# A gated MLP's two projections with their last 64 rows packed side by side, a written instruction order, and Wd's gradient split around dh

## The chip, the cores and the metric

The kernel runs on one core of one Trainium2 chip. The metric is the device time of one execution in microseconds (us); the time given for a version is the median of its runs.

## The reference, cut to what matters

The reference is the gradient of an attention block whose output is gated by a small MLP, for S = 2048 positions, D = 576 features, F = 4608 hidden features and 32 heads of 128. All tensors are bf16. The part that the change touches is the forward MLP and the gradients that belong to it:

```python
xn = _layernorm(x, axis=-1)
s = _A_ref(xn, k_cache, v_cache, wq, wo)      # attention
g = jnp.einsum("bsd,df->bsf", xn, w_gate)
u = jnp.einsum("bsd,df->bsf", xn, w_up)
h = _sigmoid(g) * u
gate = _silu(jnp.einsum("bsf,fd->bsd", h, w_down))
out = x + s * gate
```

The outputs are `out` and the gradients with respect to x, the two caches, wq, wo, w_gate, w_up and w_down.

## The kernel before

Everything runs on one core, stage after stage. D = 576 is four full tiles of 128 and a rest of 64 (`DT` = 5 tiles, `DL` = 4 full ones, `KL` = 64). The rest tile is padded: `zpad` (L158 to 160) clears rows 64 to 127 of the fifth tile of `xnT`, `wg_sb` and `wu_sb`, so that its matmul can use all 128 rows of the array, half of them with zeros.

**Stage 1, the projections (L177 to 263).** The 2048 positions are 16 row blocks (`st`). Each is layer-normed by `ln_tile` (L206 to 221): VectorE's statistics over two halves (L211, L213), a square root on ScalarE (L215), a reciprocal and a bias on VectorE (L216, L219), the normalisation itself on ScalarE (L220), and five TensorE transposes (L59) whose result is copied to `xnT` by VectorE (the four full tiles) and ScalarE (the rest). F is nine chunks of 512 in three groups of three. For each group, each row block and each chunk, a *unit* computes g and u: five matmuls of 128x512 into a PSUM bank for g (L249) and five for u (L252). ScalarE then makes sigmoid(g) (`a_row`, L253) and sigmoid(-g) (`oma`, L255); VectorE makes h = u * a (L256) and b = h * oma (L257). After three chunks the rows h, a and b are stored to DRAM from Pool's DMA queue (L259, L262, L263). There are 144 units. PSUM has three pairs of banks for them. Rows and small tiles have two or three buffers.

Loads of x and the weights are issued on SP (L183, L194, L195, L197): the first two row blocks of x, the first chunk of both weights, the other 14 row blocks in one transfer, then the rest of group 0 and groups 1 and 2. Wd's load (`wd_sb`, L236) and the store of the normed x (L235) are written at the last row block of group 0. The order of the instructions on each engine is the scheduler's here, which may move an instruction ahead of where it is written.

**Stage 2 (L267 to 325)** multiplies h, read back transposed (`hT`, L261 and L282), with Wd (L306). It reads the last tile of `xnT`, whose upper half (rows 64 to 127) it overwrites with the transposed rest of another tensor (`transpose_ds`). Then the **attention stage** runs over the heads, by far the longest, with an order written by hand for TensorE, VectorE and ScalarE. A stage over the row blocks follows (L723), and its transposes `transpose_doB` (L669).

**The stage of the MLP's weight gradients (L740 to 825)** goes over 18 blocks of 256 hidden features (`fb`). In each, `make_dh` (L776) computes dh and from it `du_blk` and `dg_blk` on VectorE (L781, L782); `make_dwd` (L794) computes two tiles of Wd's gradient (`fl` 0 and 1) from `h_blk` and `doB`; then come the gradients of Wu and Wg (`accw`, L811) and, for their last 64 rows, `accl` (L819), which puts du's into columns 0 to 63 of the array and dg's into columns 64 to 127. In the first block make_dwd goes ahead of make_dh, with the last three `transpose_doB` inside it; in the others it is the other way round. `load_abh` loads h, a and b of a block, `h_blk` on Pool's queue except for the first block. Only SP keeps its written order in this stage. The scheduler puts the first 20 matmuls of dh ahead of the first dWd tile in the first block.

Of the kernel before, what the change touches and what calls it, by code (L numbers as in the profile page):

```python
# [9 lines left out]
bf = mybir.dt.bfloat16  # L10
# [3 lines left out]
P = 128  # L14
# [81 lines left out]
def kernel(  # L96
# [77 lines left out]
    zpad(xnT)  # L174
    dsT = pk.tile([P, DL, S], bf, name="dsT")
    wo_h = pk.tile([P, D], bf, name="wo_h")
    with tc.tile_pool(name="pa", bufs=1) as pa:  # L177
        wd_sb = pa.tile([P, FT, D], bf, name="wd_sb")
        with tc.tile_pool(name="a1w", bufs=1) as wp:
            a0x = tc.alloc_tile_pool(name="a0x", bufs=1, side="right")  # L180
            x_all = a0x.tile([P, NT, D], bf, name="x_all")
            XF = min(2, NT)
            nc.sync.dma_start(x_all[:, 0:XF, :], x2[0:XF * P, :].rearrange("(t p) d -> p t d", p=P))  # L183
            xn_st = x_all
# [5 lines left out]
            bounds = [0, FCH] + list(range(WSPL, F + 1, WSPL)) if WSPL > FCH else list(range(0, F + 1, WSPL))  # L190
            for bi in range(len(bounds) - 1):
                c0, c1 = bounds[bi], bounds[bi + 1]
                for i, (d0, kd) in enumerate(dts):
                    nc.sync.dma_start(wg_sb[:kd, i, c0:c1], B_w_gate[d0:d0 + kd, c0:c1])  # L194
                    nc.sync.dma_start(wu_sb[:kd, i, c0:c1], B_w_up[d0:d0 + kd, c0:c1])  # L195
                if bi == 0 and NT > XF:
                    nc.sync.dma_start(x_all[:, XF:, :], x2[XF * P:, :].rearrange("(t p) d -> p t d", p=P))  # L197
# [4 lines left out]
            with tc.tile_pool(name="a0", bufs=3) as sb0, tc.tile_pool(name="a0ps", bufs=2, space=PSUM) as ps0, \  # L202
                    tc.tile_pool(name="a1r", bufs=2) as rows, tc.tile_pool(name="a1t", bufs=3) as tmpp, \
                    tc.tile_pool(name="a1ps", bufs=3, space=PSUM) as ps:

                def ln_tile(st):  # L206
                    xt = x_all[:, st, :]
                    stats = sb0.tile([P, nchunk, nc.vector.BN_STATS_DIM], f32, name="stats")
                    xr = xt.rearrange("p (c f) -> p c f", c=nchunk)
                    for c in range(nchunk):  # L210
                        nc.vector.bn_stats(stats[:, c, :], xr[:, c, :])  # L211
                    mv = sb0.tile([P, nc.vector.BN_AGGR_DIM], f32, name="mv")
                    nc.vector.bn_aggr(mv[:], stats[:])  # L213
                    std = sb0.tile([P, 1], f32, name="std")
                    nc.scalar.activation(std[:], mv[:, 1:2], AF.Sqrt, bias=eps_t[:], scale=1.0)  # L215
                    nc.vector.reciprocal(rstd_all[:, st:st + 1], std[:])  # L216
                    xn_t = xn_st[:, st, :]
                    nbias = sb0.tile([P, 1], f32, name="nbias")
                    nc.vector.scalar_tensor_tensor(nbias[:], mv[:, 0:1], -1.0, rstd_all[:, st:st + 1], op0=ALU.mult, op1=ALU.mult)  # L219
                    nc.scalar.activation(xn_t, xt, AF.Identity, bias=nbias[:], scale=rstd_all[:, st:st + 1])  # L220
                    transpose_to(nc, ps0, xn_t, D, xnT, st * P, ident, alt)

                LA = 2
                for st in range(min(LA, NT)):
                    ln_tile(st)
                for grp in range(NFC // GRP):
                    if grp == 1:
                        a0x.release()
                        hp0 = tc.alloc_tile_pool(name="a2h0", bufs=1, side="right", reuse_waits="tile")
                        hT = {k: hp0.tile([P, FT, P], bf, name=f"hT{k}") for k in range(2)}  # L230
                    for st in range(NT):
                        if grp == 0 and st + LA < NT:
                            ln_tile(st + LA)
                        if grp == 0 and st == NT - 1:
                            nc.gpsimd.dma_start(xn_d[:, :].rearrange("(t p) d -> p t d", p=P), xn_st[:])  # L235
                            nc.gpsimd.dma_start(wd_sb[:], B_w_down.rearrange("(t p) d -> p t d", p=P))  # L236
                        srows = slice(st * P, (st + 1) * P)
                        a_row = rows.tile([P, GRP * FCH], bf, name="a_row")
                        b_row = rows.tile([P, GRP * FCH], bf, name="b_row")
                        h_row = rows.tile([P, GRP * FCH], bf, name="h_row")  # L240
                        for c in range(GRP):
                            fc = grp * GRP + c
                            fs = slice(fc * FCH, (fc + 1) * FCH)
                            cs = slice(c * FCH, (c + 1) * FCH)
                            g_ps = ps.tile([P, FCH], f32, name="g_ps")
                            u_ps = ps.tile([P, FCH], f32, name="u_ps")
                            for i, (d0, kd) in enumerate(dts):
                                kk = kfull(i, kd)
                                nc.tensor.matmul(g_ps[:], lhsT=xnT[:kk, i, srows], rhs=wg_sb[:kk, i, fs], start=(i == 0), stop=(i == DT - 1))  # L249
                            for i, (d0, kd) in enumerate(dts):  # L250
                                kk = kfull(i, kd)
                                nc.tensor.matmul(u_ps[:], lhsT=xnT[:kk, i, srows], rhs=wu_sb[:kk, i, fs], start=(i == 0), stop=(i == DT - 1))  # L252
                            nc.scalar.activation(a_row[:, cs], g_ps[:], AF.Sigmoid)  # L253
                            oma = tmpp.tile([P, FCH], bf, name="oma")
                            nc.scalar.activation(oma[:], g_ps[:], AF.Sigmoid, scale=-1.0)  # L255
                            nc.vector.tensor_tensor(h_row[:, cs], u_ps[:], a_row[:, cs], op=ALU.mult)  # L256
                            nc.vector.tensor_tensor(b_row[:, cs], h_row[:, cs], oma[:], op=ALU.mult)  # L257
                        cols = slice(grp * GRP * FCH, (grp + 1) * GRP * FCH)
                        nc.gpsimd.dma_start(h_d[srows, cols], h_row[:])  # L259
                        if grp == NFC // GRP - 1 and st in hT:  # L260
                            nc.sync.dma_start_transpose(hT[st][:], h_d[srows, :])  # L261
                        nc.gpsimd.dma_start(a_d[srows, cols], a_row[:])  # L262
                        nc.gpsimd.dma_start(b_d[srows, cols], b_row[:])  # L263

# [395 lines left out]
    if True:  # L660
# [80 lines left out]
        with tc.tile_pool(name="b1o", bufs=2, reuse_waits="tile") as outp, tc.tile_pool(name="b1t", bufs=3, reuse_waits="tile") as tmpp, \  # L741
# [21 lines left out]
            for fb in range(F // FB):  # L763
# [22 lines left out]
                def make_dwd():  # L786
                    for fl in range(FB // P):
                        frows = slice(fb * FB + fl * P, fb * FB + (fl + 1) * P)
                        accs = [psa.tile([P, 512], f32, name=f"accd{j}") for j in range(len(ncs))]
                        for st in range(NT):  # L790
                            if (fl, st) in ((0, NT // 2), (1, 4), (1, 12)) and pend_tr:
# [196 lines left out]
```

## Time and profile before

| what | value |
|---|---|
| median of 3 runs | 5172.25 us (5167.11 to 5178.84) |
| the profiled execution, its own time | 5193.94 us |
| span of the profiled execution | 5192.2 us |
| mean granted TensorE clock | 0.993 |
| TensorE busy | 5002.7 us (96%) |
| weight loads | 3622.5 us (70%) |
| VectorE busy | 3251.7 us (63%) |
| ScalarE busy | 2293.4 us (44%) |
| Pool busy | 1448.0 us (28%) |

How to read it: the span is that of one execution taken by the hardware profiler, and all rows of the trace are times inside it, counted from its start. PE is TensorE, PEld its weight loads, DVE VectorE, ACT ScalarE, POOL GpSimd, SP the engine that only issues DMAs; a q behind a name means the issuing of a DMA. L with a number is a line of the kernel. A row of the order of time gives start, duration, engine, line, operation, output and inputs; neighbours of one kind are merged, "x4" being their number. Matmuls are pipelined, so the durations of neighbours overlap, and the distance between two starts is the time that one takes of the engine. A few per cent of the matmul records are missing from a trace, so counts come from the code. In square brackets stands how long the engine was idle ahead of the row and what ended it.

### The profile page before, as it was taken

The page shows a single profiled execution, that of the slowest core. Times are in us where ns is not written, and L with a number is a line of the kernel's source. Part 1 is how long each engine was busy: PE and PEld are TensorE (multiplying, and loading weights), DVE is VectorE, ACT ScalarE, POOL GpSimd, SP SyncE. Part 2 cuts the span into 40 slices and gives each one's busy share as a digit, 9 for nine tenths or more (in the row PEclk, how much of TensorE's full clock was granted, in tenths as well). Part 3 has the DMA queues.
Part 4 walks back from the last instruction along what each step waited for, and adds up shares of the span by engine and source line. Part 5 has one row for each costly group of instructions (what it writes and reads, how often), then busy time and mean ns, then how long its engine had stood idle before and what let it go on. Part 6 is the DMA issues. An engine that isn't in the chain of part 4 may idle for free.

```text
span 5192.2 us, 127341 instructions
## 1 busy us (share of the span) xinstructions
PE 5002.7 (96%) x54402; PEld 3622.5 (70%) x55312; DVE 3251.7 (63%) x5099; ACT 2293.4 (44%) x2922; POOL 1448.0 (28%) x2110
## 2 busy tenths in 40 slices
PE   7999999999999999999999999999899999999999
PEld 3444777777777777777777777777757777754554
DVE  4545887888888888888888888888733222210111
ACT  6541665565566556655655665565501222100000
POOL 2222233233233323322332333233222333211000
PEclk8999999999999999999999999999999999999999
DMA  7477999999999999999999999999999776697775
GB/s 270 183 214 167 188 193 193 198 199 196 193 198 196 188 202 199 195 196 191 197 196 197 197 196 200 196 194 199 208 197 248 202 202 190 200 242 162 154 148 122
DMA packets 2712489, 1013.48 MB, mean 195 GB/s; under 512 B 2525424, under 2 KB 2646000, under 8 KB 2711920
## 3 DMA queue, kind: packets, MB, share of 16 engines
q1 hardware_dynamic: 2628256, 726.57, 81.3%
q0 software_dynamic: 83664, 278.71, 18.2%
q8 instruction: 432, 7.08, 0.6%
q14 instruction: 137, 1.12, 0.1%
HBM read 172.54 MB, written 201.00 MB: 72 GB/s over the span
## 4 chain that ended last, share of the span: by engine, by line
PE 84%; DMA 6%; DVE 5%; issue 4%; SPq 0%; ACT 0%; DVEq 0%; ACTq 0%; another core or an unknown queue 0%
PE acckv L544 17%; PE acc L525 14%; PE acc L929 7%; PE dp L495 6%; PE sp L465 5%; PE accw L811 5%; PE accp L424 4%; DVE sneg L467 4%; PE u_ps L252 3%; PE dh L776 3%; PE g_ps L249 3%; DMA dST<-dSq 3%; PE acc L306 3%; PE accd L794 3%; PE acc L867 2%
## 5 line engine op out<-in xcount | busy, mean ns | idle before, releaser
L476 ACT ACTIVATE Pq<-sneg,nm 128x2048 bf16<-128x2048 bf16 x512 | 1024.5, 2001 | 391.6 <-DVE sneg L467 388.5
L525 PE MATMUL acc<-Kn,dST 128*128 128x128 bf16 x8192 | 1068.5, 220 | 31.6 <-DMA dST<-dSq 29.8
L544 PE MATMUL acckv<-dOn,Pq 128*128 128x128 bf16 x8192 | 1032.7, 219 | 15.2
L525 PE MATMUL acc<-Vn,PT 128*128 128x128 bf16 x8192 | 1023.2, 219 | 14.7 <-DMA PT<-Pq 12.9
L498 DVE SCALAR_TENSOR_TENSOR dSq<-dp,delta,Pq 128x1024 bf16<-128x1024 f32 x608 | 774.2, 1281 | 361.9 <-PE dp L495 253.0
L544 PE MATMUL acckv<-Qn,dSq 128*128 128x128 bf16 x8192 | 899.5, 220 | 8.5 <-issue 0.2
L525 PEld LDWEIGHTS <-dST 128*128 128x128 bf16 x8192 | 759.6, 98 | 167.4 <-DMA dST<-dSq 38.3
L544 PEld LDWEIGHTS <-Pq 128*128 128x128 bf16 x8192 | 793.6, 98 | 117.1 <-issue 0.5
L525 PEld LDWEIGHTS <-PT 128*128 128x128 bf16 x8192 | 766.1, 98 | 156.0 <-DMA PT<-Pq 17.3
L544 PEld LDWEIGHTS <-dSq 128*128 128x128 bf16 x8192 | 721.0, 98 | 100.3 <-issue 1.1
L467 DVE TENSOR_SCALAR_CACHE_REDUCE sneg<-sp,nm 128x1024 bf16<-128x1024 f32 x512 | 656.6, 1282 | 83.3 <-PE sp L465 46.6
L467 DVE TENSOR_SCALAR_CACHE_REDUCE sneg<-sp 128x1024 bf16<-128x1024 f32 x512 | 625.3, 1221 | 59.4 <-PE sp L465 41.8
L501 ACT ACTIVATE t<-dp,negdelta 128x1024 bf16<-128x1024 f32 x416 | 463.6, 1114 | 431.1 <-PE acc L525 242.7
L465 PE MATMUL sp<-KT,QT 128*128 128x512 bf16 x1763 | 547.2, 379 | 33.2 <-DVE sneg L467 26.4
L495 PE MATMUL dp<-VT,dOT 128*128 128x512 bf16 x1728 | 541.5, 380 | 0.5 <-DVE dSq L498 0.5
L484 POOL TENSOR_TENSOR dOn<-dOn,rinv_all 128x256 bf16<-128x256 bf16 x256 | 155.9, 609 | 658.8 <-DVE rinv_all L480 541.7
L505 DVE TENSOR_TENSOR dSq<-t,Pq 128x1024 bf16<-128x1024 bf16 x416 | 319.4, 768 | 0.0
L811 PEld LDWEIGHTS <-xn_all 128*128 128x128 bf16 x2304 | 225.0, 98 | 31.6 <-DMA xn_all<-xn_d 3.1
L929 PEld LDWEIGHTS <-cf 128*128 128x128 bf16 x2304 | 145.9, 98 | 143.5 <-DMA cf<-dg_d 5.0
L942 DVE SCALAR_TENSOR_TENSOR junk<-dxn,xn_all 128x576 f32<-128x576 f32 x16 | 12.1, 758 | 372.8 <-ACT dxn L937 372.8
L591 POOL DMA_DIRECT2D dq_d<-dq_n x128 | 98.7, 771 | 478.6 <-DVE dq_n L590 470.2
L465 PEld LDWEIGHTS <-QT 128*128 128x128 bf16 x2048 | 163.1, 98 | 52.6 <-issue 50.8
(182 smaller groups left out, 6925.0 us busy)
## 6 DMA issues: line engine op xcount, KB each, us to landing
out_dram<-kv POOLq DMA_DIRECT2D x256, 128.0 KB, 5.0
h_d<-h_row POOLq DMA_DIRECT2D x48, 384.0 KB, 2.7
a_d<-a_row POOLq DMA_DIRECT2D x48, 384.0 KB, 2.6
b_d<-b_row POOLq DMA_DIRECT2D x48, 384.0 KB, 3.2
a_blk<-a_d SPq DMA_DIRECT2D x18, 1024.0 KB, 5.8
b_blk<-b_d SPq DMA_DIRECT2D x18, 1024.0 KB, 21.8
du_d<-du_blk POOLq DMA_DIRECT2D x18, 1024.0 KB, 8.4
dg_d<-dg_blk POOLq DMA_DIRECT2D x18, 1024.0 KB, 11.5
```

The lines of the kernel that those rows point to most:

```text
L424: nc.tensor.matmul(acc[:], lhsT=w[:, i, :], rhs=srcT[:, i, cs], start=(i == 0), stop=False)
L465: nc.tensor.matmul(sp[:, c * CH:(c + 1) * CH], lhsT=hs.QT[:, qs], rhs=hs.KT[:, hf * HW_ + c * CH: hf * HW_ + (c + 1) * CH], start=True, st ...
L467: nc.vector.tensor_scalar(sneg[:, hf * HW_:(hf + 1) * HW_], sp[:], -SCALE, None if hf == 0 else nm[:, hf - 1:hf], op0=ALU.mult, op1=ALU.mi ...
L476: nc.scalar.activation(Pq[:], sneg[:], AF.Exp, bias=nm[:, hf:hf + 1], scale=-1.0, accum_out=hs.rs_all[:, qt:qt + 1])
L495: nc.tensor.matmul(dp[:, c * CH:(c + 1) * CH], lhsT=hs.dOT[:, qs], rhs=hs.VT[:, hf * HW_ + c * CH: hf * HW_ + (c + 1) * CH], start=True, s ...
L498: nc.vector.scalar_tensor_tensor(dSq[:, hsl], dp[:], hs.delta[:, qt:qt + 1], Pq[:, hsl], op0=ALU.subtract, op1=ALU.mult)
L501: nc.scalar.activation(t[:], dp[:], AF.Identity, bias=hs.negdelta[:, qt:qt + 1], scale=1.0)
L505: nc.vector.tensor_tensor(dSq[:, hsl], t[:], Pq[:, hsl], op=ALU.mult)
L525: nc.tensor.matmul(bx.acc[:, j, :], lhsT=T[qt][:, kt, :], rhs=getattr(hs, rhs)[:, kt, :], start=(kt == 0), stop=(kt == NT - 1))
L544: nc.tensor.matmul(bx.acc[i][:, jj, :], lhsT=slabs[qt][:, k0:k0 + P], rhs=getattr(hs, rhs)[:, qt, :], start=(qt == 0 and jj == 0), stop=(q ...
L811: nc.tensor.matmul(acc[:kd, :FB], lhsT=xn_all[:, st, d0:d0 + kd], rhs=blk_[:, st, :], start=(st == 0), stop=(st == NT - 1))
L929: nc.tensor.matmul(accs[sl][j][:, :nn], lhsT=ch[:, kk, sl * P:(sl + 1) * P], rhs=w_[:, n0:n0 + nn], start=(pi == 0 and kk == 0), stop=(las ...
```

## The change

1. **Row packing.** The weights' fifth tiles go into one tensor `wl_sb`: rows 0 to 63 hold Wg's last 64 rows, rows 64 to 127 Wu's. The fifth tile of `xnT` holds the last 64 features twice, made by copying them twice side by side (`xl`) ahead of a 128-wide transpose. Units go in pairs: `full` of the first (eight matmuls), `rest` of the first and of the second (two matmuls each, g's on rows 0 to 63 and u's on rows 64 to 127), `full` of the second. The padding memsets go.
2. **Written order.** All five engines keep the order in which stage 1 is written. Statistics, square roots, norms and transposes stand at unit numbers (`stats_at`, `do`); the square roots are taken for 2, 2, 4, 4 and 4 row blocks at once. The first six units go chunk by chunk over two row blocks.
3. **Norms on Pool.** From the third row block on Pool normalises; it makes `xl` as well. One VectorE copy of five tiles moves each transposed row block to `xnT`.
4. **Loads.** SP loads group 0's weights in three chunks with x in pieces of 2, 2, 4 and 8 row blocks between them. The ten transfers of group 1's weights are issued on Pool's queue, one after each row block's stores in group 0, those of group 2 in group 1, and Wd in nine parts in the row blocks that are left.
5. **Buffers.** Three for the rows h, a, b instead of two, two for `oma` instead of three.
6. **First dWd.** In the first block of the weight-gradient stage the order is dWd's tile 0, dh, dWd's tile 1; all three late `transpose_doB` are in tile 0. The scheduler again puts 20 matmuls of dh ahead, and the other 60 between the two tiles.

Cut to its core:

```diff
-            wg_sb = wp.tile([P, DT, F], bf, name="wg_sb")
-            wu_sb = wp.tile([P, DT, F], bf, name="wu_sb")
-            zpad(wg_sb)
-            zpad(wu_sb)
+            wg_sb = wp.tile([P, DL, F], bf, name="wg_sb")
+            wu_sb = wp.tile([P, DL, F], bf, name="wu_sb")
+            wl_sb = wp.tile([P, F], bf, name="wl_sb")
...
+                def ln_norm(st):
+                    rstd, nbias = rstd_all[:, st:st + 1], nb_all[:, st:st + 1]
+                    if st < LA:
+                        nc.scalar.activation(x_all[:, st, :], x_all[:, st, :], AF.Identity, bias=nbias, scale=rstd)
+                    else:
+                        nc.gpsimd.tensor_scalar(x_all[:, st, :], x_all[:, st, :], rstd, nbias, op0=ALU.mult, op1=ALU.add)
+                    xl[st] = sb0.tile([P, 2, KL], bf, name="xl", bufs=2)
+                    nc.gpsimd.tensor_copy(xl[st][:], x_all[:, st, D - KL:].unsqueeze(1).to_broadcast([P, 2, KL]))
...
+                stats_at = {0: 2, 1: 3, 2: 4, 4: 5, 5: 6, 6: 7, 10: 8, 12: 9, 14: 10, 15: 11, 22: 12, 24: 13, 26: 14, 27: 15}
+                for k, t0, t1 in ((1, 2, 4), (7, 4, 8), (16, 8, 12), (28, 12, NT)):
+                    do(k, ln_rstd, t0, t1)
+                for st in range(2, NT):
+                    do(GRP * (st - 2) + 1 if st > 3 else st, ln_norm, st)
+                    do(-1 - (GRP * (st - 1) + (st == 4) if st > 3 else st + 2), ln_tr, st)
...
+                def full(k, first):
+                    for p_, w_ in zip(banks[k], (wg_sb, wu_sb)):
+                        for i in range(DL):
+                            nc.tensor.matmul(p_[:], lhsT=xnT[:, i, st * P:(st + 1) * P], rhs=w_[:, i, fs],
+                                             start=(first and i == 0), stop=(not first and i == DL - 1))
+                def rest(k, first):
+                    for j, p_ in enumerate(banks[k]):
+                        rs = slice(j * KL, (j + 1) * KL)
+                        nc.tensor.matmul(p_[:], lhsT=xnT[rs, DL, st * P:(st + 1) * P], rhs=wl_sb[rs, fs], start=first, stop=not first)
...
+                    if k % 2 == 0:
+                        full(k, True)
+                        rest(k, False)
+                        rest(k + 1, True)
+                    else:
+                        full(k, False)
...
+                        if st >= 1 and w_late.get(grp):
+                            nc.gpsimd.dma_start(*w_late[grp].pop(0))
+                        elif st >= 1 and wd_parts and grp < NFC // GRP - 1:
+                            ft = wd_parts.pop(0)
+                            nc.gpsimd.dma_start(wd_sb[:, ft, :], B_w_down.rearrange("(t p) d -> p t d", p=P)[:, ft, :])
...
-                for fn in ((make_dwd, make_dh) if fb == 0 else (make_dh, make_dwd)):
-                    fn()
+                if fb == 0:
+                    make_dwd(0)
+                    make_dh()
+                    make_dwd(1)
+                else:
+                    make_dh()
+                    for fl in range(FB // P):
+                        make_dwd(fl)
```

More of the change, by code (lines that the diff above doesn't have):

```diff
@@ L202 @@
             with tc.tile_pool(name="a0", bufs=3) as sb0, tc.tile_pool(name="a0ps", bufs=2, space=PSUM) as ps0, \
[L203 to L209, printed above, removed]
+                    tc.tile_pool(name="a1r", bufs=3) as rows, tc.tile_pool(name="a1t", bufs=2) as tmpp, \
@@ L218, in ln_tile @@
[L218 to L221, printed above, removed]
-                LA = 2
[L224 to L236, printed above, removed]
-                        srows = slice(st * P, (st + 1) * P)
[L238 to L257, printed above, removed]
```

112 lines of the change are left out of this document (91 added, 21 removed).

## The prediction

> **What bounds the kernel now.** I read the page's head, slices and chain first, then the busy times by stretch over the first stage, then the order of time on TensorE there.
>
> ```profile
> span 5192.2 us, 127341 instructions
> PE   7999999999999999999999999999899999999999
> PEclk8999999999999999999999999999999999999999
> PE 84%; DMA 6%; DVE 5%; issue 4%; SPq 0%; ACT 0%; DVEq 0%; ACTq 0%; another core or an unknown queue 0%
> ```
>
> TensorE is 84% of the chain that ended last, and every slice of PE but one is at 8 or 9. The one that is not, slice 1 (the first 130 us), has the only granted clock under 9 too. So time is won by giving TensorE fewer slots of work, or by removing its idle start. The change does both in the stage of the gate and up projections, so that stage is cut into stretches:
>
> ```profile
> core 0: us, PE busy (x) PEld busy (x) DVE busy (x) ACT busy (x) POOL busy (x), PEclk, DMA share, GB/s
> 10.00:20.00 10.00, 2.47 (x6) 0.76 (x5) 1.92 (x7) 3.03 (x5) 2.97 (x2) 0.80 1.05 361
> 20.00:30.00 10.00, 4.47 (x9) 1.15 (x9) 4.56 (x17) 4.04 (x5) 0.00 (x0) 0.50 1.04 350
> 30.00:40.00 10.00, 6.01 (x17) 2.21 (x17) 2.58 (x15) 1.92 (x4) 0.00 (x0) 0.50 1.03 336
> 40.00:60.00 20.00, 16.71 (x81) 7.82 (x82) 13.29 (x45) 17.74 (x32) 3.76 (x7) 0.92 1.03 358
> 160.00:357.40 197.40, 196.45 (x899) 89.46 (x915) 101.73 (x183) 99.69 (x184) 48.38 (x91) 1.00 0.56 194
> ```
>
> The last row is the steady part: TensorE without a gap at clock 1.00, VectorE and ScalarE half busy. From 10 to 40 us it is the other way round: 32 matmuls in 30 us, clock down to 0.50, DMA share above 1.
>
> ```profile
> 8.45 1.89 PE L249 MATMUL g_ps<-wg_sb,xnT 128*128 128x512 bf16 x4
> 50.30 1.24 PE L252 MATMUL u_ps<-wu_sb,xnT 128*128 128x512 bf16 x5
> 55.70 0.78 PE L59 MATMUL pt<-ident,x_all 128*128 128x128 bf16 x7
> 357.36 17.80 PE L306 MATMUL acc<-wd_sb,hT 128*128 128x512 bf16 x141
> 48.72 0.56 PE L59 MATMUL pt<-ident,x_all 128*128 128x128 bf16 x5
> 49.21 1.04 PE L249 MATMUL g_ps<-wg_sb,xnT 128*128 128x512 bf16 x4
> ```
>
> The stage runs from 8.45 to 357.36, 348.9 us. Between 50.30 and 55.70 lie five groups of five matmuls: 5.40 / 25 = 0.216 us a slot. There are 144 units (3 groups x 16 rows x 3 chunks) of ten slots: 1440 x 0.216 = 311.0. Fourteen rows have their transposes inside the stage, 49.21 - 48.72 = 0.49 each: 6.9. What is left, 348.9 - 311.0 - 6.9 = **31.0 us, is lost at the start**. The next rows tell why.
>
> ```profile
> 10.98 1.99 POOL L236 DMA_DIRECT2D wd_sb<-in_B_w_down_dram  x1
> 18.08 1.18 DVE L211 BATCH_NORM_STATS2 stats<-x_all 128x6 f32<-128x288 bf16 x3 [9.10 <-DMA x_all<-in_A_x_dram]
> PE g_ps L249 <- DMA wg_sb<-in_B_w_gate_dram: 12.4, 3, 8.2
> ```
>
> Wd's load was written for the last row of group 0, but nothing held it back and it was issued at 10.98; its 4608 x 576 values, 5184 KB, then share the DMA engines with 14 row blocks of x in one transfer (2016 KB, landed about 18) and the weights of all three groups. TensorE waits for the second piece of Wg, 8.2 us at once, and its clock falls.
>
> **The change, part by part.**
>
> *Row packing.* Five matmuls for g and five for u become four and four of 128 rows, and the last 64 rows of both side by side: g's in rows 0 to 63 of the array, u's in rows 64 to 127. Units go in pairs, so that four half matmuls (g, u of one, g, u of the next) stand together. If the halves run at once these four take two slots, and a pair takes (16 + 2) x 0.216 = 3.89 instead of 20 x 0.216 = 4.32. No matmul of before uses half the rows; the nearest is half the columns, in the dWg/dWu stage:
>
> ```profile
> 4511.95 0.60 PE L811 MATMUL accw<-dg_blk,xn_all 128*128 128x256 bf16 x4
> 4512.48 0.30 PE L819 MATMUL accl<-du_blk,xn_all 128*64 128x256 bf16 x1
> 4512.48 0.30 PE L819 MATMUL accl<-dg_blk,xn_all 128*64 128x256 bf16 x1
> 4512.61 0.27 PE L819 MATMUL accl<-du_blk,xn_all 128*64 128x256 bf16 x1
> 4514.03 0.27 PE L819 MATMUL accl<-du_blk,xn_all 128*64 128x256 bf16 x1
> 4514.14 0.27 PE L819 MATMUL accl<-du_blk,xn_all 128*64 128x256 bf16 x1
> 4514.35 0.88 PE L867 MATMUL acc<-ds_all,onb 128*128 128x512 bf16 x4
> ```
>
> Two things to see. The du and dg halves start at the same instant, and the next two 0.11 us later (4514.03, 4514.14): halves do run at once. And going in and out costs: the last whole matmul began at 4511.95 + 0.60 - 0.27 = 4512.28, the first half one 0.20 later; the last half one is followed after 0.21; a slot here is 0.11. With 0.02 more inside (4512.61 - 4512.48 = 0.13), a visit costs 0.09 + 0.10 + 0.02 = about 0.22 beyond its slots. I take 0.22 for rows as well: 72 x 0.22 = 15.8. The bounds are no cost, and 0.43, which eats the two slots saved. So: 72 x 3.89 = 279.9, plus 15.8.
>
> The Trainium skill, "TensorEngine Tiling (Array Packing)", Key Properties, says that changing the tiling mode drains the TensorE; it is the rule that speaks against this change. It gives no figure; by it the 0.22 is right in kind, and the rows above agree for columns; no run shows rows yet. With no drain the sum would be 15.8 us lower.
>
> *Transposes.* The 64-wide fifth transpose becomes a 128-wide one of a doubled column block.
>
> ```profile
> 3922.67 0.72 PE L669 MATMUL pt<-ident,doB 128*128 128x128 bf16 x10
> 3923.23 0.38 PE L776 MATMUL dh<-wdT,doBT 128*128 128x256 bf16 x2
> ```
>
> Ten whole transposes take 0.56, so five take 0.28 and not 0.49: 14 x 0.28 = 3.9, saving 3.0. One VectorE copy takes the place of VectorE's and ScalarE's.
>
> *The start.* SP now brings only group 0's weights in three chunks, with x in four pieces between them; groups 1 and 2 and Wd go on Pool's queue, one transfer a row.
>
> ```profile
> 4.00:6.00 2.00, 0.00 (x0) 0.00 (x0) 1.84 (x8) 0.57 (x3) 2.00 (x1) 1.00 0.87 249
> 1.24 0.46 SPq L194 DMA_DIRECT2D wg_sb<-in_B_w_gate_dram  x1
> 5.68 0.58 SPq L195 DMA_DIRECT2D wu_sb<-in_B_w_up_dram  x1
> wu_sb<-in_B_w_up_dram SPq DMA_DIRECT2D x4, 128.0 KB, 3.7
> ```
>
> Ten issues lie between 1.24 and 5.68, 0.49 apart, and land 3.7 later. Of the new order the 22nd issue ends chunk 1 and the 33rd chunk 2: about 11.5 and 17 us, landed by 15.2 and 20.7. By bytes, 2.95 and 4.72 MB at 249 GB/s from 2 us on: 13.8 and 21.0. TensorE starts at 8.5 as before. Its first row above has 0.42 a slot (1.89 - 0.63 over three); with 16 slots so, 3.4 us are lost to the clock. It wants the end of chunk 1 at 8.5 + 4.1 + 3.4 + 1.7 = 17.7 and of chunk 2 at 21.8. So the transfers are just ahead. I leave 8 us for all losses (3.4, and 4.6 for the hiccups below), between 3 and the 31.0 of now.
>
> *LayerNorm and the written order.* All five engines now keep the written order. The terms:
>
> ```profile
> L256 DVE TENSOR_TENSOR h_row<-u_ps,a_row 128x512 bf16<-128x512 f32 x143 | 98.8, 691 | 134.4 <-ACT oma L255 115.2 <-PE u_ps L252 8.7 <-ACT a_row L253 8.6
> L257 DVE TENSOR_TENSOR b_row<-h_row,oma 128x512 bf16<-128x512 bf16 x143 | 60.7, 424 | 15.6 <-DMA b_d<-b_row 3.0
> L42 DVE COPY xnT<-pt 128x512 bf16<-128x512 bf16 x16 | 6.7, 419 | 9.6 <-PE pt L59 9.5
> L320 POOL CAST g2b<-g 128x1152 bf16<-128x1152 f32 x8 | 13.8, 1722 | 66.7 <-DVE g L312 66.6
> L484 POOL TENSOR_TENSOR dOn<-dOn,rinv_all 128x256 bf16<-128x256 bf16 x256 | 155.9, 609 | 658.8 <-DVE rinv_all L480 541.7 <-DVE dOn L42 116.9
> L259 POOL DMA_DIRECT2D h_d<-h_row x48 | 26.0, 542 | 69.3 <-DVE h_row L256 69.3
> L215 ACT ACT_TABLE_LOAD x8 | 10.3, 1283 | 0.8 <-PEq L972 0.7
> ```
>
> Pool's norm of 576 elements is not shown: at the cast's 1.5 ns an element 0.9 us, at the product's 2.4 ns 1.4 us. I take 1.4, plus 0.3 for the doubled block. Four issues of 0.54 make a row 3.9 of the 6.15 us that three units take. The norm stands behind the row's three stores and a weight load in Pool's queue, and behind the last b_row; it ends some 3 us before TensorE reaches the transposes, about 1 us where rstd of four rows has just been made. A square root in ScalarE's queue costs two table loads, 2.6 us, four times; the a_row behind them is late, and TensorE has two units of banks in hand (4.1 us). VectorE in group 0 has 48 x 1.115 for h and b, and 14 times two statistics at 0.39 and a copy of 640 at 0.52, with small operations some 1.5: 75 of 102 us, plus some 10 behind the square roots. So the cover holds, narrowly: 4.6 us for what does not. If it were gone, each row pays what it is late, up to the bound above.
>
> The Trainium skill, "SBUF — State Buffer", Who interferes with whom, says that a VectorE instruction with two SBUF inputs and a GpSimd one that reads SBUF block each other. By it b_row would wait for a norm, at most 1.4 us in 14 rows, within the cover; no row of before has the two together.
>
> *Three row buffers* take away waits of 3.0 us on VectorE, off TensorE's path: nothing. *Wd* is there by the middle of the stage either way, needed at its end: nothing.
>
> *dWd around dh.*
>
> ```profile
> PE accw L811 <- DMA xn_all<-xn_d: 2.8, 1, 2.8
> ```
>
> Before accw TensorE does the same work in another order, so it still arrives early for xn_all. But h_blk's next load, which waits for the last accd, is issued later and leaves its bandwidth to xn_all: between 2.8 won and 0.5 lost (dh earlier, with b_blk still to land). I take 1.
>
> **Sum.** 279.9 + 15.8 + 3.9 + 8 = 307.6 for 348.9: 41.3 less. With dWd 42.3, taken as **42**. Everything behind the stage follows from its end, so it moves as a block. The profiled execution took 5193.94 (1.7 outside its span), 0.4% above the median of 5172.25; the sum gives 5152 for it and **5130** for the median.
>
> **The rivals.**
>
> *A: the halves do not run at once.* Then 20 slots and the visit: 4.32 + 0.22 = 4.54 a pair, 72 x 0.43 = 31 more: 5161. The accl rows speak against it, but they are columns.
>
> *B: the start is not mended*, because 33 small transfers on SP, or the chain square root, norm, transposes, copy, keep TensorE waiting: all 31.0 lost as now, 23 more: 5153. For it: 0.49 an issue, and 1 us in hand at places. Against: 10.5 MB that competed from 10 to 40 us are gone.
>
> *C: slower.* Each change between the two halves costs what going in or out costs, 0.11, and they run one after another: four slots and five changes, 0.86 + 0.55 = 1.41 a visit where the forecast has 0.65 and before had 0.86. 72 x 0.76 = 55 more: 5185. From 0.65 + 42 / 72 = 1.23 us a visit on, the change loses. Against it: accl alternates between halves at 0.11 a pair for 16 pairs.
>
> *D: changing to half rows costs nothing*: 16 less, 5114.
>
> **How the numbers follow.** Forecast 0.66, A 0.10, B 0.13, C 0.05, D 0.06. The forecast alone spans 5118 to 5142. The range goes from 5112, which holds D, to 5156, which holds B; A and C stay outside. About 0.2% is what a measurement of this kernel tells from no change: 10 us, so faster is below 5162. Forecast, B and D are faster, and somewhat over half of A, whose 5161 lies on the bound: 0.90. Same: the rest of A, 0.04, and a little of C: 0.05. Slower: 0.05.
>
> **What would show it.** Right: L306 first starts near 316 us, not 357; granted clock 1.00 from about 16 us on; pairs of the 64-row matmuls start together, and from one pair of units to the next lie 4.1 us in groups 1 and 2. A would show 4.5 there, C 4.9, D 3.9. B would show waits of TensorE for wg_sb, wl_sb or xl and a clock of 0.50 after 20 us. The accw wait for xn_all should be under 2.8. What makes it wrong: any wait of TensorE for VectorE or Pool in every row of group 0.

## The result and the profile after

The changed kernel takes 5123.59 us (median of 4 runs) where the one before takes 5175.55: a ratio of 0.9893, 95% interval 0.9867 to 0.9919. Five further rounds of the same kernel gave 5126.15 and 0.9913 (0.9891 to 0.9934). The profiled execution took 5131.98, its span is 5130.2: 62.0 us less than the one of before. The forecast was 5130 with 42 us won.

First the stretches of stage 1 in the profile after; the columns are those of the same view of before.

```profile
core 0: us, PE busy (x) PEld busy (x) DVE busy (x) ACT busy (x) POOL busy (x), PEclk, DMA share, GB/s
10.00:20.00 10.00, 9.63 (x39) 3.31 (x39) 4.31 (x12) 5.57 (x9) 1.28 (x3) 1.00 0.85 253
20.00:30.00 10.00, 9.30 (x52) 3.95 (x53) 9.28 (x23) 6.31 (x13) 4.75 (x9) 1.00 0.84 288
30.00:40.00 10.00, 9.95 (x54) 3.92 (x54) 7.27 (x18) 6.82 (x12) 4.80 (x9) 1.00 0.85 279
```

From 10 to 40 us TensorE now starts 145 matmuls where it started 32, at clock 1.00, and the DMA share is 0.85 instead of above 1. Next the order of time on TensorE, at the start, for one pair of units late in the stage, and at the stage's end.

```profile
8.77 1.89 PE L280 MATMUL g_ps<-wg_sb,xnT 128*128 128x512 bf16 x4
...
12.30 0.60 PE L288 MATMUL g_ps<-wl_sb,xnT 64*128 64x512 bf16 x1
...
296.25 1.03 PE L280 MATMUL u_ps<-wu_sb,xnT 128*128 128x512 bf16 x4
297.21 0.39 PE L288 MATMUL g_ps<-wl_sb,xnT 64*128 64x512 bf16 x1
297.21 0.39 PE L288 MATMUL u_ps<-wl_sb,xnT 64*128 64x512 bf16 x1
297.44 0.38 PE L288 MATMUL g_ps<-wl_sb,xnT 64*128 64x512 bf16 x1
297.44 0.38 PE L288 MATMUL u_ps<-wl_sb,xnT 64*128 64x512 bf16 x1
297.75 1.04 PE L280 MATMUL g_ps<-wg_sb,xnT 128*128 128x512 bf16 x4
...
301.31 0.39 PE L288 MATMUL g_ps<-wl_sb,xnT 64*128 64x512 bf16 x1
...
311.77 3.56 PE L377 MATMUL acc<-wd_sb,hT 128*128 128x512 bf16 x26
```

Stage 1 runs from 8.77 to 311.77: 303.0 us instead of 348.9. g's and u's half matmul start at the same instant. From one visit to half rows to the next (297.21 to 301.31) lie 4.10 us, the forecast's number for a pair. Inside the pair: four whole slots end at 296.25 + 4 x 0.216 = 297.11 and the first halves start 0.10 later; the second halves come after 0.23 instead of 0.216; the next whole matmul after 0.31 instead of 0.216. A visit costs 0.10 + 0.01 + 0.09 = 0.20 beyond its slots.

What TensorE still waits for in stage 1 (engine, line, releaser, us in total, times, longest):

```profile
PE g_ps L280 <- issue: 1.7, 11, 0.2
PE g_ps L280 <- DMA wg_sb<-in_B_w_gate_dram: 1.0, 3, 0.4
PE g_ps L288 <- ACT oma L314: 0.3, 1, 0.3
```

No wait is left that is longer than 0.4 us. So the stage's 45.9 us divide as follows. The slots and visits are 72 x 4.10 = 295.2 for 311.0: 15.8. The transposes, at 0.29 (22.73 to 23.02 in the same order of time), are 4.1 for 6.9: 2.8. The rest, 303.0 - 295.2 - 4.1 = 3.7 us, is what the start loses, instead of 31.0: **27.3**. The other 16 us of the 62.0 lie behind stage 1; the experiments come back to them.

### The profile page after: what moved, and what is told of

It reads as the page before. It is cut to its first block, busy times and chain, and to the rows that moved or that the text cites. A ratio compares the mean times of both kernels' runs of the same rounds, so it can differ in the third digit from the quotient of the medians.

```text
span 5130.2 us, 127328 instructions
## 1 busy us (share of the span) xinstructions
PE 4970.7 (97%) x54403; PEld 3593.9 (70%) x55312; DVE 3252.2 (63%) x5077; ACT 2268.8 (44%) x2875; POOL 1473.0 (29%) x2165
## 4 chain that ended last, share of the span: by engine, by line
PE 84%; DVE 6%; issue 5%; DMA 4%; POOL 1%; SPq 1%; ACT 0%; DVEq 0%; POOLq 0%; ACTq 0%
PE acckv L615 17%; PE acc L596 15%; PE acc L1006 8%; PE dp L566 7%; PE sp L536 5%; PE accw L888 5%; PE accp L495 5%; DVE sneg L538 4%; PE dh L847 3%; PE acc L377 3%; PE accd L865 3%; PE acc L944 2%; PE acct L502 2%; PE acc L794 2%; PE accq L953 2%
## 5 line engine op out<-in xcount | busy, mean ns | idle before, releaser
L538 DVE TENSOR_SCALAR_CACHE_REDUCE sneg<-sp,nm 128x1024 bf16<-128x1024 f32 x512 | 656.4, 1282 | 83.4 <-PE sp L536 45.9
L280 PEld LDWEIGHTS <-xnT 128*128 128x128 bf16 x1152 | 107.1, 98 | 147.2 <-issue 30.9
```

Source lines behind the costliest of these rows:

```text
L538: nc.vector.tensor_scalar(sneg[:, hf * HW_:(hf + 1) * HW_], sp[:], -SCALE, None if hf == 0 else nm[:, hf - 1:hf], op0=ALU.mult, op1=ALU.mi ...
```

## The experiments

The theory: the gain is the start (27 us, by what no longer competes with group 0's weights and x) and the packing (16 us, less than its two slots a pair because each visit to half rows costs 0.20); the transposes' 2.8 come beside them. The rivals: the packing alone, the start alone, or something that the later stages gained. Since single executions differ by some 20 us, most verdicts below go by the length of stage 1, from the first g matmul to the first matmul on hT; where the total was timed it is given.

### The changed kernel again

> The changed kernel once more, unedited. Theory: stage 1 (first g_ps matmul to first matmul of the next stage) takes 303 us again within 1, and the first accw starts without a wait; the other 16 us by which the two profiled executions differ (62.0 us of span against 45.9 in stage 1 and 2.8 in the first dWd block) are mostly the attention stage's waits for its DMA transposes, which vary between executions, so attention (first sp to last sp matmul) should come out several us away from its 3185. Rival: the change shortens attention itself; then it stays at 3185 within 2.

Stage 1 took 302.4, and the first accw did not wait. From the first sp matmul to the last lie 3189.8 us, 4.8 more than in the first profile. Both parts of the theory hold.

### The kernel before again

> The kernel before once more, unedited. Theory: stage 1 takes 348 to 350 again; the three stages from the first sp matmul to the first accd, 3412 us in the first profile, lie between 3396 and 3412 in nine profiles of other versions whose code there is the same, so they should come out anywhere in that range. Rival (the change shortens these stages too): 3410 or more again.

Rows of the first sp and the first accd matmul (count, durations in ns, first and last start), of before and of before again:

```profile
L465 PE MATMUL sp<-KT,QT x1763: 376/379/544, 514.5 to 3709.1; 128*128 128x512 bf16 x196
L794 PE MATMUL accd<-doB,h_blk x1116: 192/193/380, 3926.5 to 4498.4; 128*128 128x64 bf16 x149, 128*128 128x512 bf16 x37
```

```profile
L465 PE MATMUL sp<-KT,QT x1763: 376/379/634, 508.2 to 3680.1; 128*128 128x512 bf16 x196
L794 PE MATMUL accd<-doB,h_blk x1116: 192/193/380, 3905.2 to 4472.4; 128*128 128x64 bf16 x149, 128*128 128x512 bf16 x37
```

From the first sp to the first accd: 3412.0 in the one and 3397.0 in the other, the same kernel. In the changed kernel it was 3401.4 and 3408.5; in the eight kernels edited from the changed one 3396 to 3407, in the two edited from before 3412 and 3413. So these stages differ by up to 16 us between executions, and the 10.6 us that the first pair of profiles shows there need no cause in the change. Whether a small systematic part is in it, these 14 profiles do not settle. The theory missed in one point: stage 1 took 342.5, not 348 to 350. The long start of before varies too: with 342.5 it loses 24.6 us instead of 31.0. By the two profiles of each kernel the change's gain in stage 1 is 40 to 46 us.

### Without the packing

```diff
-            wl_sb = wp.tile([P, F], bf, name="wl_sb")
+            wl_g = wp.tile([P, F], bf, name="wl_g")
+            wl_u = wp.tile([P, F], bf, name="wl_u")
+            wl_ = (wl_g, wl_u)
+            nc.gpsimd.memset(wl_g[KL:, :], 0.0)
+            nc.gpsimd.memset(wl_u[:KL, :], 0.0)
...
-                    tc.tile_pool(name="a1r", bufs=3) as rows, tc.tile_pool(name="a1t", bufs=2) as tmpp, \
+                    tc.tile_pool(name="a1r", bufs=2) as rows, tc.tile_pool(name="a1t", bufs=2) as tmpp, \
...
-                        nc.tensor.matmul(p_[:], lhsT=xnT[rs, DL, st * P:(st + 1) * P], rhs=wl_sb[rs, fs], start=first, stop=not first)
+                        nc.tensor.matmul(p_[:], lhsT=xnT[:, DL, st * P:(st + 1) * P], rhs=wl_[j][:, fs], start=first, stop=not first)
```

> The changed kernel without the packing: the last 64 rows of Wg and of Wu are padded to 128 again, each in a tensor of its own, and two row buffers instead of three make room. Theory: a pair of units takes 20 x 0.216 = 4.32 instead of 4.10, so stage 1 takes 72 x 0.22 = 16 us more, 319, and the start stays mended. Rival (the packing brings nothing, all the gain is the start): 303 to 305. Rival (the packing is nearly all of it): 340 or more.

Stage 1 took 324.2, the total 5163.97 (ratio to before 0.9976, 0.9954 to 0.9997). Of the 5 us over the forecast 319, one wait explains them:

```profile
PE g_ps L291 <- ACT oma L317: 5.5, 1, 5.5
```

Without it 318.7. The wait belongs to the two row buffers and not to the padding: ScalarE had just waited 10.6 us for the store of an earlier `a_row`. So in stage 1 the packing is worth 16 us, a third of the stage's gain; the rest is there without it. The timed totals lie further apart: 5163.97 is 38 us above the changed kernel's 5126.15, each of the two ratios being known to about 11 us, where stage 1 accounts for 21 to 22. No profile shows what the rest is, if it is more than chance.

### One visit per unit, and one per row block

```diff
-                    if k % 2 == 0:
-                        for k_ in (k, k + 1):
-                            banks[k_] = [ps.tile([P, FCH], f32, name=nm) for nm in ("g_ps", "u_ps")]
-                        full(k, True)
-                        rest(k, False)
-                        rest(k + 1, True)
-                    else:
-                        full(k, False)
+                    banks[k] = [ps.tile([P, FCH], f32, name=nm) for nm in ("g_ps", "u_ps")]
+                    full(k, True)
+                    rest(k, False)
```

> Each unit does its own two half-row matmuls after its eight whole ones: 144 visits instead of 72, the same number of slots. Theory (a visit costs 0.20 to 0.22): stage 1 takes 72 x 0.2 = 14.5 to 16 us more, 317.5 to 319, as long as without the packing. Rival (a visit is free and something else fills the 4.10 us): 303.

Stage 1 took 317.5, 14.5 more for 72 more visits: 0.20 each. The total was 5151.0 (0.9962, 0.9945 to 0.9979). With a visit in each unit the packing saves nothing against whole rows (318.7): the one slot saved, 0.216, is about what the visit costs.

```diff
+                    n = 2 if k < LA * GRP else GRP
-                    if k % 2 == 0:
-                        for k_ in (k, k + 1):
+                    if k % n == 0:
+                        for k_ in range(k, k + n):
                             banks[k_] = [ps.tile([P, FCH], f32, name=nm) for nm in ("g_ps", "u_ps")]
                         full(k, True)
                         rest(k, False)
-                        rest(k + 1, True)
+                        for k_ in range(k + 1, k + n):
+                            rest(k_, True)
```

> From the seventh unit on, the half-row matmuls of all three units of a row block stand together (six in a visit), so 46 visits take the place of 69. Theory (a visit to half rows costs 0.20 to 0.22 us beyond its slots, whatever number of half matmuls it holds): stage 1 takes 23 x 0.2 = 4.6 to 5 us less than 303, about 298.4, the whole kernel 5 less than the changed kernel. Rival (the cost is in each change between the halves): no change, 303. A second rival: the three pairs of banks do not come free in time, and TensorE waits up to 0.8 us in each row: 303 or more.

Order of time on TensorE, from one visit to the next:

```profile
291.17 0.39 PE L288 MATMUL g_ps<-wl_sb,xnT 64*128 64x512 bf16 x1
...
291.39 0.38 PE L288 MATMUL g_ps<-wl_sb,xnT 64*128 64x512 bf16 x1
...
291.61 0.38 PE L288 MATMUL g_ps<-wl_sb,xnT 64*128 64x512 bf16 x1
...
291.92 1.04 PE L280 MATMUL g_ps<-wg_sb,xnT 128*128 128x512 bf16 x4
...
297.20 0.39 PE L288 MATMUL g_ps<-wl_sb,xnT 64*128 64x512 bf16 x1
```

Three pairs of halves stand 0.22 apart, and a row block takes 297.20 - 291.17 = 6.03, less than the 1.5 x 4.10 = 6.15 of the pairs. Stage 1 took 298.7, 4.3 less than 303.0, as the price of 23 visits (4.6) says; the banks came free in time, for TensorE waited 1.0 us in all for ScalarE. The total, 5123.61 (0.9916, 0.989 to 0.9942), lies 2.5 us under that of the changed kernel timed beside it, less than either is known. By the trace it is the better version, by the timed total it is not told apart.

### Both halves on the same rows

```diff
-            wl_sb = wp.tile([P, F], bf, name="wl_sb")
+            wl_g = wp.tile([KL, F], bf, name="wl_g")
+            wl_u = wp.tile([KL, F], bf, name="wl_u")
+            wl_ = (wl_g, wl_u)
...
-                        rs = slice(j * KL, (j + 1) * KL)
-                        nc.tensor.matmul(p_[:], lhsT=xnT[rs, DL, st * P:(st + 1) * P], rhs=wl_sb[rs, fs], start=first, stop=not first)
+                        nc.tensor.matmul(p_[:], lhsT=xnT[:KL, DL, st * P:(st + 1) * P], rhs=wl_[j][:, fs], start=first, stop=not first)
```

> Both rests lie in rows 0 to 63 of the array (Wu's in a tensor of its own, two row buffers instead of three): the four half matmuls of a visit cannot run side by side. Theory: four slots and the visit, 20 x 0.216 + 0.2 = 4.52 a pair, stage 1 303 + 72 x 0.43 = 334. Rival (two halves on the same rows overlap as well, since each needs only part of the array): 303.

```profile
323.77 0.39 PE L289 MATMUL g_ps<-wl_g,xnT 64*128 64x512 bf16 x1
324.00 0.38 PE L289 MATMUL u_ps<-wl_u,xnT 64*128 64x512 bf16 x1
324.22 0.38 PE L289 MATMUL g_ps<-wl_g,xnT 64*128 64x512 bf16 x1
324.43 0.38 PE L289 MATMUL u_ps<-wl_u,xnT 64*128 64x512 bf16 x1
324.74 1.04 PE L282 MATMUL g_ps<-wg_sb,xnT 128*128 128x512 bf16 x4
```

The four now start one after another, about 0.22 apart. From one visit to the next lie 4.52 us (319.25 to 323.77), as forecast, and stage 1 took 331.4 where 334 was expected; one execution took 5155.58. It is different rows that let them run at once. The sequence goes in and out of half rows once, whatever the halves are, and costs no more inside.

### Wd: held back, first, and in pieces

The kernel before, with Pool alone kept in written order:

```diff
-                    tc.tile_pool(name="a1ps", bufs=3, space=PSUM) as ps:
+                    tc.tile_pool(name="a1ps", bufs=3, space=PSUM) as ps, \
+                    tc.manual_schedule(engines={mybir.EngineType.Pool}):
```

> The kernel before with one edit: Pool keeps the written order in stage 1, so Wd's load is issued at the last row block of group 0 and not at 11 us. Theory: of the 10.5 MB that were moved from 10 to 40 us 5.3 are gone; x's long transfer and the second piece of the weights (5.8 MB with the first) are there near 19 us instead of 40, so of the 31 us lost at the start 12 to 22 come back, and stage 1 takes 327 to 337 instead of 348.9. Rival (x in one transfer and the weights of groups 1 and 2 on SP are the cause, Wd only fills the queue): at least 344.

Stage 1 took 349.2 and the whole 5170.45 (0.9994, 0.9971 to 1.0017): not the theory's 327 to 337. It is in the rival's range, 344 or more, but not for the rival's reason, for much of the start was mended. Two stretches of this kernel, the same two of before, and what ScalarE waits for in this kernel in the second of them:

```profile
20.00:40.00 20.00, 17.78 (x92) 8.36 (x92) 13.21 (x41) 13.39 (x24) 3.22 (x6) 1.00 1.04 340
140.00:160.00 20.00, 5.27 (x24) 2.33 (x24) 0.18 (x1) 0.60 (x2) 1.55 (x3) 0.74 1.00 367
```

```profile
20.00:40.00 20.00, 10.49 (x26) 3.36 (x26) 7.14 (x31) 5.96 (x9) 0.00 (x0) 0.50 1.04 343
140.00:160.00 20.00, 19.89 (x92) 9.11 (x93) 10.54 (x20) 9.77 (x18) 4.84 (x9) 1.00 0.48 188
```

```profile
ACT a_row L254 <- DMA a_d<-a_row: 20.5, 1, 20.5
```

From 20 to 40 us TensorE starts 92 matmuls instead of 26, 66 x 0.216 = 14 us won. From 140 to 160 it starts 24 instead of 92, and 68 x 0.216 = 15 us are given back: Wd's 5 MB and the store of xn now stand on Pool's queue between the row stores, and ScalarE cannot write a row of the two buffers before its store has landed. It waits 20.5 us for that. So one transfer of Wd costs some 15 us where it was written as well; that it is Wd and not the store of xn the next kernel shows, where xn's store stands at the same place. From this came the next kernel, Wd in nine pieces between the row stores of group 1:

```diff
-                            nc.gpsimd.dma_start(wd_sb[:], B_w_down.rearrange("(t p) d -> p t d", p=P))
...
+                        if grp == 1 and 0 < st < 10:
+                            wt = slice(4 * (st - 1), 4 * st)
+                            nc.gpsimd.dma_start(wd_sb[:, wt, :], B_w_down.rearrange("(t p) d -> p t d", p=P)[:, wt, :])
```

> The kernel before with Pool's order kept (as in wd_held) and Wd in nine pieces of four tiles, one after the stores of row blocks 1 to 9 of group 1; nothing else is changed. Theory formed after wd_held (Wd in one transfer costs about 15 us wherever it stands, at the start by delaying x and the weights, at the end of group 0 by delaying the row stores that ScalarE waits for with two buffers): in pieces it costs nothing, and stage 1 takes 329 to 335 instead of 348.9. Rival (two row buffers wait for any transfer that stands between the stores): at least 342.

Stage 1 took 331.9, inside the range, and the total 5155.89 (0.9969, 0.9944 to 0.9993). From 140 to 160 us it starts 93 matmuls again:

```profile
140.00:160.00 20.00, 19.89 (x93) 9.03 (x93) 10.30 (x19) 9.94 (x19) 6.62 (x12) 1.00 0.76 268
```

The longest wait left to TensorE in stage 1 is for the second weight piece, behind x in one transfer:

```profile
PE g_ps L249 <- DMA wg_sb<-in_B_w_gate_dram: 5.2, 1, 5.2
```

This edit of a few lines brings 11 to 17 us of stage 1, against the two profiles of before. It is still 13 us longer than the 318.7 of the changed kernel without its packing: 5.2 are this wait, 3.7 waits for ScalarE and 2.8 the transposes. Which of the change's other parts (the order of the loads, the written order, the square roots together) takes the waits away was not tried one by one. The other side of it, the changed kernel with Wd in one transfer ahead of all else:

```diff
+                nc.gpsimd.dma_start(wd_sb[:], B_w_down.rearrange("(t p) d -> p t d", p=P))
                 LA = 2
...
-                wd_parts = [slice(i, min(i + 4, FT)) for i in range(0, FT, 4)]
+                wd_parts = []
```

> The changed kernel with Wd in one transfer, issued on Pool's queue ahead of everything in stage 1. Theory: it shares the DMA engines with the 4.7 MB that stage 1 wants by 21 us, so these land 5 to 10 us later and TensorE's clock falls again: stage 1 308 to 318 instead of 303. Rival (small pieces on SP go ahead whatever else is queued): 303 to 305.

Its first stretches, and TensorE's largest wait in stage 1:

```profile
10.00:20.00 10.00, 3.62 (x7) 0.85 (x7) 0.00 (x0) 0.44 (x1) 0.00 (x0) 1.00 1.04 349
20.00:30.00 10.00, 8.75 (x23) 2.28 (x22) 4.40 (x12) 4.59 (x7) 1.41 (x3) 1.00 0.93 295
```

```profile
PE g_ps L281 <- DMA wg_sb<-in_B_w_gate_dram: 6.4, 6, 3.9
```

7 matmuls from 10 to 20 us instead of 39, and stage 1 takes 315.0, 12 more, as the theory had it; one execution took 5143.51. Small pieces on SP do not go ahead of a long transfer on Pool's queue.

### Two row buffers

```diff
-                    tc.tile_pool(name="a1r", bufs=3) as rows, tc.tile_pool(name="a1t", bufs=2) as tmpp, \
+                    tc.tile_pool(name="a1r", bufs=2) as rows, tc.tile_pool(name="a1t", bufs=2) as tmpp, \
```

> The changed kernel with two buffers for the rows h, a, b instead of three. The prediction's step (three row buffers bring nothing): stage 1 stays at 302 to 304. Rival (in whole_rows, with two buffers, one wait of ScalarE's chain made 5.5 us; the wider queue behind Pool's extra transfers makes two buffers too few): 306 to 312, in waits of a_row for a store.

The largest waits of ScalarE and of TensorE in stage 1:

```profile
ACT a_row L312 <- DMA a_d<-a_row: 17.6, 6, 6.2
```

```profile
PE g_ps L288 <- ACT oma L314: 1.4, 1, 1.4
```

Stage 1 took 304.4, one execution 5130.73. ScalarE waits for stores 17.6 us in six times, where it waits 6.1 in two with three buffers, but the pairs of banks hide all but 1.4 us of it from TensorE. The third buffer is worth 1.4 to 2 us here, not nothing, and not what the rival said (in the kernel with whole rows, two buffers had cost 5.5).

### Norms on ScalarE

```diff
-                    if st < LA:
-                        nc.scalar.activation(x_all[:, st, :], x_all[:, st, :], AF.Identity, bias=nbias, scale=rstd)
-                    else:
-                        nc.gpsimd.tensor_scalar(x_all[:, st, :], x_all[:, st, :], rstd, nbias, op0=ALU.mult, op1=ALU.add)
+                    nc.scalar.activation(x_all[:, st, :], x_all[:, st, :], AF.Identity, bias=nbias, scale=rstd)
```

> The changed kernel with the norms of all row blocks on ScalarE (0.87 us each, 14 of them in group 0) instead of Pool. Theory (ScalarE is half busy and the written order leaves time): stage 1 stays at 302 to 305. Rival (in wd_held ScalarE was busy 19.8 of 20 us through group 0 with norms and two table loads a row; its queue is what the norms had to leave): 308 or more, in waits of TensorE for ScalarE.

Stage 1 took 302.4, one execution 5126.14: moving the norms to Pool brings nothing by itself. ScalarE is busy 57.64 of the 80 us from 20 to 100 here, and 48.67 in the changed kernel. In wd_held it was 19.8 of 20 from 60 to 80 us, with norms and two table loads in every row block. That the square roots, taken four row blocks at once, are what makes room for the norms here fits, but was not tried alone.

### dWd in the old order

```diff
                 if fb == 0:
                     make_dwd(0)
-                    make_dh()
                     make_dwd(1)
+                    make_dh()
```

> The changed kernel with the first block of the weight-gradient stage in its old order (both dWd tiles, then dh). Theory: h_blk's next load is issued early again and TensorE waits for xn_all, 1 to 3 us at the first accw; from the first accd to the first accw 16 to 17.5 us instead of 14.5. Rival (the wait went because everything came earlier, not because of the order): no wait, 14.5.

(The three late transposes go back to where before has them.) From the first accd to the first accw lie 19.0 us, and the wait is back, larger than expected:

```profile
PE accw L888 <- DMA xn_all<-xn_d: 4.5, 1, 4.5
```

One execution took 5141.38. In the old order the wait is 2.8, 0, 0.3 and 0 us in the four profiles of before and of what was edited from it, and 4.5 here; in the new order it is 0 in all nine profiles. That does not yet show that the order takes the wait away, for the executions with a wait differ before either order begins. The last microsecond before xn_all's load is issued, in before (2.8), dwd_before (4.5), before_again (0) and the changed kernel (0):

```profile
3922.30:3923.30 1.00, 1.00 (x17) 0.79 (x14) 0.46 (x1) 0.21 (x1) 0.16 (x1) 1.00 1.21 290
3872.30:3873.30 1.00, 1.00 (x16) 0.87 (x15) 0.59 (x1) 0.21 (x1) 0.30 (x1) 1.00 1.21 289
3900.90:3901.90 1.00, 1.00 (x17) 0.76 (x15) 0.44 (x1) 0.21 (x1) 0.14 (x1) 1.00 0.00 0
3866.90:3867.90 1.00, 1.00 (x17) 0.76 (x15) 0.43 (x1) 0.21 (x1) 0.14 (x1) 1.00 0.00 0
```

Where TensorE waits long, the DMA engines are still moving 290 GB/s; in wd_held, with its wait of 0.3, it is 75, and in all 11 profiles without a wait it is 0. The first block's a_blk had been issued only 7.2 us ahead of xn_all in the two with a long wait, 9.0 in wd_held, and 9.8 or more elsewhere. xn_all then lands 20.6 and 22.1 us after its issue, 18.0 in wd_held, and 16.7 to 17.2 otherwise. h_blk's next load is issued 8.3 us after the first accd in all five profiles of the old order, also in the two without a wait. So that load alone does not make the wait, and since no execution of the new order met busy DMA engines at this point, the record does not show what the order does to it. Without a wait, the first accw comes 14.4 us after the first accd in the old order and 14.5 in the new.

## Why the prediction was right

*What bounds the kernel, and the place*: right. The 31.0 us lost at the start and the slots of stage 1 were the two things to win, and 45.9 of the 62.0 us between the profiles come from there.

*Row packing*: right in mechanism and size. The visit was taken from half columns at 0.22; on half rows it is 0.20, and visits 144, 72 and 49 in number (the first three pairs keep theirs in the last) gave 317.5, 303.0 and 298.7. The Trainium skill's rule ("TensorEngine Tiling (Array Packing)", Key Properties: a change of mode drains the engine) agrees with these rows, which add the number it lacks here. Rivals A, C and D fall with the 4.10 us of a pair, where they had 4.5, 4.9 and 3.9; same_half shows that A's 4.5 does come when the halves lie on the same rows.

*Transposes*: 2.8 for the forecast 3.0.

*The start*: the mechanism was right and the size on the safe side. It loses 3.7 us where 8 had been left: about 2 for the first slots, which take twice as long (eight from 8.77 to 12.30, 0.44 each), and 1.0 in three waits for weights at 19 to 21 us, where the forecast had the transfers just ahead. The forecast put the slow slots down to the clock and counted 16 of them; the view gives a granted clock of 1.00 from 8 us on, so no run here shows why they are slow. The 4.6 us set aside for hiccups of the written order did not come: no wait of TensorE in stage 1 passed 0.4 us. The 31.0 that the sum started from are those of one profile; in before_again they are 24.6, which the forecast could not know.

*Wd*: the prediction put the start down to Wd's early load, and costed Wd's own move at nothing. wd_held shows what that left out: held back whole, it stops the row stores and gives all back. In nine pieces it takes nothing away from these stretches (93 matmuls from 140 to 160 us).

*LayerNorm*: Pool's norm, taken at 1.4 us from bounds of 0.9 and 1.4, is 0.97. Groups of instructions in the changed kernel, on Pool (up to 105 us) and on VectorE (20 to 100 us), and the VectorE group of norm_scalar (20 to 100):

```profile
L238 POOL TENSOR_SCALAR x_all<-x_all,rstd_all,nb_all 128x576 bf16<-128x576 bf16 x14 | 13.5, 968 | 13.2 <-DVE nb_all L231 12.7
```

```profile
L316 DVE TENSOR_TENSOR b_row<-h_row,oma 128x512 bf16<-128x512 bf16 x38 | 18.7, 492 | 3.8
```

```profile
L313 DVE TENSOR_TENSOR b_row<-h_row,oma 128x512 bf16<-128x512 bf16 x38 | 16.2, 426 | 3.8
```

The same instructions by their tile (shortest, median and longest in ns, first and last start), in the changed kernel and in norm_scalar:

```profile
L316 DVE TENSOR_TENSOR b_row<-h_row,oma x38: 424/426/887, 20.9 to 99.1; 128x512 bf16<-128x512 bf16 x38
```

```profile
L313 DVE TENSOR_TENSOR b_row<-h_row,oma x42: 424/426/427, 14.3 to 103.2; 128x512 bf16<-128x512 bf16 x42
```

With Pool norming, b_row takes 492 ns in the mean and 887 at most; with ScalarE norming 426 and 427. The norm is slowed as well: 0.81 us at 31.88, with no b_row beside it, and 1.10 at 41.86, beside a b_row of 0.68. That agrees with the rule of the Trainium skill, "SBUF — State Buffer", Who interferes with whom: a VectorE instruction with two inputs in SBUF and a GpSimd one that reads SBUF block each other. Its price here is 2.5 us of VectorE in 38 instructions, off TensorE's path.

*Three row buffers*: said to bring nothing; 1.4 to 2 us, of ScalarE's waits and not of VectorE's.

*dWd*: not borne out. The wait of 2.8 us is gone in the profiled pair, where 1 had been taken, but the mechanism, h_blk's load leaving its bandwidth to xn_all, is not what the traces show: the wait comes where transfers are still under way when xn_all's load is issued, and where there are none both orders are without it. That the pair agreed with the forecast here is luck.

*The sum*: 42 was forecast, and the medians differ by 52 in the first timing and 47 in the second, known to about 13 and 11 us. In stage 1 alone 41.3 was forecast and 40 to 46 came. There is luck in the closeness: the start of before was taken from its longer profile, and against that the changed kernel's start was taken 4 us too long; from 342.5 the same sum would have given 35 for stage 1. What the sum had wrong is that everything behind the stage "moves as a block": it does in the code, but its own length differs by up to 16 us between executions, and the two profiled ones happened to fall 13 us apart the same way as the change. Whether the 1 to 12 us by which the medians' differences exceed the gain of stage 1 are more than chance, the record does not settle.

## What to carry to other kernels

Packing two 64-row rests side by side saves one slot for each two matmuls, and each visit to half rows costs 0.20 us, about a slot of 512 columns here: gather as many half matmuls in a visit as PSUM banks allow, for with one pair a visit nothing is won. Look where a scheduler puts a load that nothing holds back, and at what else stands on the queue that it is moved to: a 5 MB transfer cost about the same 15 us between the row stores as ahead of the first weights, and in nine pieces no loss showed. When executions differ by more than the effect, compare the length of the stage that was edited, and run the kernel before again to see how much the other stages move by themselves.

## What was not expected of the hardware

A short wait of TensorE costs more than itself. After the 2.8 us for xn_all in the kernel before, the granted clock of the next stretch is 0.68:

```profile
3945.00:3950.00 5.00, 5.00 (x34) 3.91 (x32) 0.43 (x1) 0.37 (x1) 1.30 (x3) 0.68 1.10 355
```

From the first accw to the first matmul of the stage behind lie 570.5 us there and 571.2 in dwd_before, with its wait of 4.5; in all the others 568.8 or 568.9. The first 64 accw matmuls hold all of it: they take 8.7 and 9.3 us, and 7.0 in every other profile. So the wait cost 1.7 to 2.4 us more than its own length.
